# A long-convolution kernel that takes 17 of 32 magnitude columns by exponentials and the rest as products

## The chip, the cores and the metric

The kernel runs on one core of a Trainium2 chip. The core has five engines, each with its own queue of instructions that run in order: TensorE (PE, matrix products, with the weight load PEld beside it), VectorE (DVE), ScalarE (ACT, functions of single elements), GpSimd (POOL) and SyncE (SP, which issues DMAs). They wait for one another by semaphores. SBUF is the working memory with 128 partitions; PSUM takes PE's results and is read by ACT and DVE. The metric is the time of one execution in microseconds, the median of several.

## The reference

Two blocks follow each other on a sequence of 2048 tokens with 448 channels: a long convolution with a state-space kernel (S4D), and an MLP across the tokens. The change is in the making of the convolution's kernel K:

```python
dt = jnp.exp(log_dt)
A = -jnp.exp(log_A_real) + 1j * A_imag
C = (C_real + 1j * C_imag) * dt[:, None]
P = jnp.exp((A * dt[:, None])[:, :, None] * pos[None, None, :])
K = 2.0 * jnp.einsum("dn,dnl->dl", C, P).real
...
y = irfft(rfft(u_t, 2 * L) * rfft(K, 2 * L), 2 * L)[:, :, :L]
...
h = layernorm(x) * (1 + cb) + sb
u = gelu(einsum("bsd,sf->bdf", layernorm(h), w1) + b1)
x = x + gb * transpose(einsum("bdf,fs->bds", u, w2) + b2)
```

K is needed at 2048 positions for 448 channels with 256 states each. With a position written as l = 64 i + j (i below 32, j below 64) every term is a product of a factor in i and a factor in j, each with a magnitude (an exponential) and a phase (sine and cosine).

## The kernel before, in words

The states lie on the partitions. The channels are taken in 28 groups of 16, and each group in two halves of 128 states, so that there are 56 halves (`NHALF`), counted by `s`. For each half the kernel makes two magnitudes of 128 x 512 (16 channels times 32 columns): `mags[s][:, 0]` holds the powers 0 to 31 of the decay per position, and `mags[s][:, 1]`, with the coefficient in it, the 32 steps of 64 positions. `st_exponents` (L600) has PE make the exponents of both in PSUM (tiles `xe` and `xg`), as products of the parameters (`lex`) with the constant table `tab[:, 2]`; `st_exp` (L605) has ACT take the exponentials. `st_mag2` (L622) makes on POOL the powers 32 to 63 (`m2`): a small product `w` (the 32nd power, as the 31st times the first) and then `m2`, the first magnitude times `w`.

The sines and the exponentials need different tables on ACT. So the exponentials of 8 halves (`BATCH`) are taken together, in `window(s)` for s = 0, 8, 16 ... 48, and a step for each half follows. A step (`st_abs` L632, `st_phase` L611, `st_step` L639) has PE make the phases in `xe` and `xg`, ACT two absolute values and four sines (two of them into tiles of the tag `gs`, which has three buffers), POOL two products `G` of the second magnitude with sine and cosine (L650, L651), and DVE four products `E` of the first magnitude and of `m2` (L652 to L658). `st_kgen` (L672) then contracts E and G on PE.

The order on PE, ACT, DVE and POOL is the order in which this code runs, written out by hand; lists `dve` and `act` hold work that is put off to the next flush. In a window the loop over e has for each half: exponentials of half s + e, the exponents of the next, flushes, and other work. Which other work depends on the window. In those of s = 8 and 16 it is rows of the input transform (`u_rows`: PE products `pu`, then DVE products `yt`, L527) and up to five DVE steps per e from `chain` (L367, the coefficients of the coming groups, by the numbers in `WPACE`); in that of s = 24 columns of the same transform and chain steps; in those of s = 32, 40 and 48 pieces of the spectrum's product (`piece`, with `zx`, `zy` and `z` of L784 to L787), and all eight `st_mag2` of the batch. In the windows below 32 only two `st_mag2` fall into the window; the others stand in the steps. In window 0 POOL also copies `dsk` (L472).

The exponent table is built in `dft_tables` (L132 to L146) and loaded by three DMAs that POOL issues (L283).

Of the kernel before, what the change touches and what calls it, by code (L numbers as in the profile page):

```python
# [22 lines left out]
P = 128  # L23
# [16 lines left out]
def dft_tables():  # L40
# [91 lines left out]

    te = np.zeros((3, 64, 16, 32))
    tg = np.zeros((3, 16, 4, 16, 32))
    n = np.arange(32)
    for d in range(16):
        te[0, 2 * d : 2 * d + 2, d] = 2 * n + 1
        te[2, 2 * d : 2 * d + 2, d] = -n
        tg[0, d, 0:2, d] = n
        tg[0, d, 2:4, d] = 1  # L140
        tg[2, d, 0:2, d] = -64 * n
        tg[2, d, 2:4, d] = 1
    tg = tg.reshape(3, 16, 2, 2, 512).swapaxes(1, 2)
    tt = np.concatenate([te.reshape(3, 64, 512), tg.reshape(3, 64, 512)], 1)
    tt[1] = -tt[0]
    t["TT"] = tt.reshape(3, P, 512)  # L146
    return {k: np.ascontiguousarray(v.astype(np.float32)) for k, v in t.items()}
# [74 lines left out]
def tile_adaln_s4d_mixer(ctx, tc, i, out):  # L222
# [20 lines left out]
    with ExitStack() as es:  # L243
# [38 lines left out]
        tab = cg.tile([P, 3, 512], F32R, name="tab")  # L282
        for v in (2, 1, 0):  # L283
            G.dma_start(tab[:, v], i["TT"][v])
# [78 lines left out]
        def flush(todo):  # L363
            while todo:
                todo.pop(0)()
# [234 lines left out]
        def st_exponents(s):  # L600
            g, h = divmod(s, 2)
            phs[s] = [pph.tile([P, 512], F32, tag=nm, name=nm) for nm in ("xe", "xg")]
            halves(phs[s], lex[g % 4][:, h * P : (h + 1) * P], tab[:, 2], True, True)

        def st_exp(s):  # L605
            mags[s] = mp.tile([P, 2, 512], F32, tag="mag", name="mag")
            pm = phs.pop(s)
            for k in range(2):
                S.activation(mags[s][:, k], pm[k], AF.Exp)  # L609

# [11 lines left out]
        def st_mag2(s):  # L622
            me = v32(mags[s][:, 0])
            w = wp.tile([P, GD], F32, tag="w", name="w")
            G.tensor_tensor(w[:, :, None], me[:, :, 31:32], me[:, :, 1:2], ALU.mult)  # L625
            m2 = m2p[s >= 32 and s % BATCH > 2].tile([P, GD, 32], F32, tag="m2", name="m2")
            G.tensor_tensor(m2, me, w[:, :, None].to_broadcast([P, GD, 32]), ALU.mult)  # L627
            m2s[s] = m2
# [346 lines left out]
        def window(s):  # L975
# [9 lines left out]
            for e in range(BATCH):  # L985
# [10 lines left out]
                flush(act)  # L996
                flush(late_act)
                if s < 32:
                    more(WPACE[s // 8][e])
# [435 lines left out]
```

## Time and profile before

| | |
|---|---|
| median of 3 runs | 693.01 us (691.97 to 696.05) |
| the profiled execution, whole | 695.37 us |
| its span, first to last instruction | 693.2 us |
| mean granted PE clock | 0.958 |
| PE busy | 621.5 us (90%) |
| DVE busy | 456.7 us (66%) |
| ACT busy | 437.6 us (63%) |
| POOL busy | 269.2 us (39%), all of it before 394 us |

The shares are means over stages with different limits. The page's view of 40 equal slices (17.3 us each; a digit is the busy share in tenths) shows where they change:

```profile
PE   0878889889988779898899989999999999999997
DVE  7578799879779468685877577776622354444431
ACT  5867599788977789999973578777422332222220
POOL 6497468259368768889766300000000000000000
```

Slices 2 to 21 hold the convolution kernel and the input transform, the next two the rest of the convolution, and from the 23rd on the MLP runs, in which POOL does nothing. What the exponentials cost stands in the view by groups (line, engine, operation, tile, count | busy us in total, mean ns of one | idle time of the engine before them, and what ended it):

```profile
L609 ACT ACTIVATE mag<-xg 128x512 f32<-128x512 f32 x56 | 35.9, 641 | 1.2 <-PE xe L598 1.2
L609 ACT ACTIVATE mag<-xe 128x512 f32<-128x512 f32 x56 | 35.7, 637 | 15.1 <-PE xe L598 6.2 <-PE pu L524 4.1 <-POOL w L625 2.0
```

Durations of neighbours on one engine overlap by some 0.1 us; the time that an instruction takes in its queue is read from one start to the next.

### The profile page before, as it was taken

To read this page: it belongs to the slowest core of one execution; us is meant where nothing else is said; L and a number is where in the kernel's file an instruction comes from. 1 tells how busy PE (TensorE), PEld (TensorE's weight loads), DVE (VectorE), ACT (ScalarE), POOL (GpSimd) and SP (SyncE) were. 2 spreads that over 40 slices of the span, in tenths; PEclk is the share of its full clock that TensorE was granted. 3 is DMA by queue.
4 is the path that set the end of the run, shared out by engine and by line. 5 is a ranking of instruction groups with operands and counts; after the bars stand their busy time and mean duration, and the time that the engine had idled before them with its cause. 6 is when DMAs were issued, how large, how long until landed. Compare 5 with 4: busy or idle time off the path is not lost. (4 is left out here: it accounts for less than half of the span.)

```text
span 693.2 us, 18255 instructions
## 1 busy us (share of the span) xinstructions
PE 621.5 (90%) x7180; PEld 462.5 (67%) x7180; DVE 456.7 (66%) x880; ACT 437.6 (63%) x876; POOL 269.2 (39%) x323
## 2 busy tenths in 40 slices
PE   0878889889988779898899989999999999999997
PEld 0444445545535556565567757778999999999996
DVE  7578799879779468685877577776622354444431
ACT  5867599788977789999973578777422332222220
POOL 6497468259368768889766300000000000000000
PEclk9997979899999989899999999999999999999999
DMA  7694646567895526444248799965674445556540
GB/s 173 195 194 110 219 163 217 208 203 233 252 298 170 156 72 159 128 132 146 84 128 261 245 269 264 243 152 149 168 242 112 141 132 160 160 159 170 167 129 27
DMA packets 104275, 121.14 MB, mean 175 GB/s; under 512 B 12858, under 2 KB 92254, under 8 KB 104062
## 3 DMA queue, kind: packets, MB, share of 16 engines
q1 hardware_dynamic: 102830, 113.92, 56.8%
q0 software_dynamic: 1360, 6.06, 4.1%
q8 instruction: 57, 0.93, 0.6%
q14 instruction: 28, 0.23, 0.1%
HBM read 84.59 MB, written 34.87 MB: 172 GB/s over the span
## 5 line engine op out<-in xcount | busy, mean ns | idle before, releaser
L207 ACT CAST whi<-w 128x896 fp32r<-128x896 f32 x64 | 59.7, 938 | 131.7 <-PE o L1402 84.6
L650 POOL TENSOR_TENSOR G<-mag,gs 128x512 f32<-128x512 f32 x56 | 72.3, 1290 | 73.2 <-ACT gs L646 70.7
L216 DVE TENSOR_TENSOR wlo<-w,whi 128x896 fp32r<-128x896 f32 x64 | 68.0, 1086 | 40.3 <-ACT whi L207 31.0
L1332 PE MATMUL acc<-h3h,whi 128*128 128x448 f32 x224 | 83.3, 372 | 1.4 <-ACT h3h L1237 1.4
L681 PEld LDWEIGHTS kg<-E,G 128*32 128x32 f32 x3584 | 59.1, 118 | 36.5 <-issue 16.4
L1334 PE MATMUL acc<-h3h,wlo 128*128 128x448 f32 x224 | 82.0, 366 | 0.0
L1333 PE MATMUL acc<-h3l,whi 128*128 128x448 f32 x224 | 81.6, 364 | 0.2 <-DVE mean L1186 0.2
L1401 PE MATMUL o<-uh,whi 128*128 128x448 f32 x224 | 81.4, 363 | 0.0
L1403 PE MATMUL o<-uh,wlo 128*128 128x448 f32 x224 | 81.2, 363 | 0.0
L1402 PE MATMUL o<-ul,whi 128*128 128x448 f32 x224 | 80.7, 360 | 0.0
L598 PE MATMUL xg<-tab,lph 64*128 64x512 f32 x112 | 67.4, 604 | 11.6 <-DVE E L658 7.2
L681 PE MATMUL kg<-E,G 128*32 128x64 f32 x3584 | 69.4, 233 | 8.9 <-issue 4.1
L598 PE MATMUL xe<-tab,lph 64*128 64x512 f32 x112 | 66.9, 600 | 9.7 <-ACT gs L647 7.0
L651 POOL TENSOR_TENSOR G<-mag,gs 128x512 f32<-128x512 f32 x56 | 71.6, 1278 | 0.0
L1405 DVE SCALAR_TENSOR_TENSOR y<-o,b,mod 128x448 f32<-128x448 f32 x16 | 11.0, 685 | 80.2 <-PE o L1403 80.2
L627 POOL TENSOR_TENSOR m<-mag,w 128x512 f32<-128x512 f32 x56 | 59.7, 1066 | 4.6 <-POOL w L625 0.3
L652 DVE TENSOR_TENSOR E<-m,xe 128x512 f32<-128x512 f32 x56 | 38.0, 679 | 28.4 <-ACT xe L645 24.5
L1332 PEld LDWEIGHTS acc<-h3h,whi 128*128 128x128 f32 x224 | 42.5, 190 | 13.6 <-ACT h L1242 6.3
L598 PE MATMUL xe<-tab,lex 64*128 64x512 f32 x56 | 32.0, 584 | 18.4 <-POOL dsk L472 17.2
L635 ACT ACTIVATE ab<-xe 128x512 f32<-128x512 f32 x56 | 34.0, 607 | 20.4 <-PE xe L598 11.2
L609 ACT ACTIVATE mag<-xe 128x512 f32<-128x512 f32 x56 | 35.7, 637 | 15.1 <-PE xe L598 6.2
L1334 PEld LDWEIGHTS acc<-h3h,wlo 128*128 128x128 f32 x224 | 42.5, 190 | 3.3
(236 smaller groups left out, 1470.3 us busy)
## 6 DMA issues: line engine op xcount, KB each, us to landing
w<-in_B_w_dram SPq DMA_DIRECT2D x64, 224.0 KB
w<-in_B_w_dram SPq DMA_DIRECT2D x32, 448.0 KB
yu_d<-yt SPq DMA_DIRECT2D x16, 448.0 KB
yi<-yu_d SPq DMA_DIRECT2D x16, 448.0 KB
us_d<-uo SPq DMA_DIRECT2D x16, 448.0 KB
u<-us_d SPq DMA_DIRECT2D x32, 224.0 KB
v_d<-vt SPq DMA_DIRECT2D x32, 224.0 KB
vt<-v_d SPq DMA_DIRECT2D x14, 448.0 KB
```

What stands on the lines that cost most here:

```text
L207: self.nc.scalar.copy(hi, w)
L216: eng.tensor_tensor(lo, w, hi.bitcast(F32), ALU.subtract)
L598: T.matmul(out[k], lhs[r], rhs[r], start=start, stop=stop)
L650: G.tensor_tensor(Gt[:, 1], mg_, v32(sg), ALU.mult)
L651: G.tensor_tensor(Gt[:, 0], mg_, v32(cg_), ALU.mult)
L681: T.matmul(kgs[g][32 * q : 32 * q + 32, m], Gt[:, c, d], E[:, c, d], start=h == 0 and c == 0 and m == 0, stop=h == 1 and c == 1, skip_grou ...
L1332: nc.tensor.matmul(acc[f], hi[:, fs], h3h[:, r], start=r == 0, stop=False)
L1333: nc.tensor.matmul(acc[f], hi[:, fs], h3l[:, r], start=False, stop=False)
L1334: nc.tensor.matmul(acc[f], lo[:, fs], h3h[:, r], start=False, stop=r == 15)
L1401: nc.tensor.matmul(o, hi[:, ks], uh[kh][:, k], start=kh == 0 and k == 0, stop=False)
L1402: nc.tensor.matmul(o, hi[:, ks], ul[kh][:, k], start=False, stop=False)
L1403: nc.tensor.matmul(o, lo[:, ks], uh[kh][:, k], start=False, stop=kh == 1 and k == 6)
```

## The change

Only columns 0 to 16 of each magnitude come from exponentials. PE makes 16 x 17 = 272 exponents instead of 512 (table `TX` in the place of the third part of `TT`), and ACT writes 17 of every 32 columns. A new function, `st_fill`, makes columns 17 to 31 of both magnitudes in one product: columns 1 to 15 times the 16th power, which is column 16 of the first magnitude. For the second magnitude, whose step is 64 positions, the 16th power is the decay over 1024 positions; column 0 of the first magnitude is used to hold it (its exponent is 1024 times the decay) until a memset puts the 1 there that belongs there. The fills stand in the window, behind the flushes of each e: on POOL in the windows of s = 8, 16 and 24 and for the odd halves of window 0, on DVE elsewhere, 28 on each. `w` becomes the square of the 16th power.

```diff
@@ dft_tables
+    tx = np.zeros((P, 16, 17))
+    k = np.arange(17)
+    for d in range(16):
+        tx[2 * d : 2 * d + 2, d] = -np.where(k > 0, k, 1024)
+        tx[64 + 2 * d : 66 + 2 * d, d] = -64 * k
+        tx[96 + 2 * d : 98 + 2 * d, d] = 1
+    t["TX"] = tx.reshape(P, 16 * 17)
...
         tab = cg.tile([P, 3, 512], F32R, name="tab")
-        for v in (2, 1, 0):
+        G.dma_start(tab[:, 2, 0 : 17 * GD], i["TX"])
+        for v in (1, 0):
             G.dma_start(tab[:, v], i["TT"][v])
...
             phs[s] = [pph.tile([P, 512], F32, tag=nm, name=nm) for nm in ("xe", "xg")]
-            halves(phs[s], lex[g % 4][:, h * P : (h + 1) * P], tab[:, 2], True, True)
+            n = 17 * GD
+            halves([t[:, 0:n] for t in phs[s]], lex[g % 4][:, h * P : (h + 1) * P], tab[:, 2, 0:n], True, True)
...
             for k in range(2):
-                S.activation(mags[s][:, k], pm[k], AF.Exp)
+                to, src = v32(mags[s][:, k])[:, :, 0:17], pm[k][:, 0 : 17 * GD]
+                S.activation(to, src.rearrange("p (d j) -> p d j", j=17), AF.Exp)
+
+        def st_fill(s, eng):
+
+            m = mags[s].rearrange("p k (d j) -> p k d j", j=32)
+            by = m[:, 0, :, 16::-16].rearrange("p d k -> p k d")
+            to, src = m[:, :, :, 17:32], m[:, :, :, 1:16]
+            eng.tensor_tensor(to, src, by[:, :, :, None].to_broadcast([P, 2, GD, 15]), ALU.mult)
+            eng.memset(m[:, 0, :, 0:1], 1.0)
...
-            G.tensor_tensor(w[:, :, None], me[:, :, 31:32], me[:, :, 1:2], ALU.mult)
+            G.tensor_tensor(w[:, :, None], me[:, :, 16:17], me[:, :, 16:17], ALU.mult)
...
                 flush(dve)
                 flush(act)
                 flush(late_act)
+                st_fill(s + e, G if 0 < s < 32 or s + e in (1, 3, 5, 7) else V)
                 if s < 32:
                     more(WPACE[s // 8][e])
```

The order of instructions moves in two places that matter. First POOL's queue in the window of s = 8, before: the rows of the input are scaled (`xt`), and w and m2 of the first two halves follow, the second pair behind two more rows.

```order
L514 TENSOR_SCALAR xt<-xt,rs,nm 128x448 x4
L625 TENSOR_TENSOR w<-mag 128x16
L627 TENSOR_TENSOR m_976<-mag,w 128x512
L514 TENSOR_SCALAR xt<-xt,rs,nm 128x448 x2
L625 TENSOR_TENSOR w<-mag 128x16
L627 TENSOR_TENSOR m_1034<-mag,w 128x512
L650 TENSOR_TENSOR G<-mag,gs 128x512
```

The same place with the change. Line numbers are those of the new file: L625 and L626 are the fill and its memset, L642 and L644 w and m2, L667 the first G.

```order
L521 TENSOR_SCALAR xt<-xt,rs,nm 128x448 x4
L625 TENSOR_TENSOR mag<-mag 128x32x15
L626 MEMSET mag 128x16
L642 TENSOR_TENSOR w<-mag 128x16
L644 TENSOR_TENSOR m_994<-mag,w 128x512
L521 TENSOR_SCALAR xt<-xt,rs,nm 128x448 x2
L625 TENSOR_TENSOR mag<-mag 128x32x15
L626 MEMSET mag 128x16
L642 TENSOR_TENSOR w<-mag 128x16
L644 TENSOR_TENSOR m_1054<-mag,w 128x512
```

A fill stands ahead of each w, and six more fills with their memsets stand between the last m2 and the first G, where nothing stood.

Second DVE's queue in the window of s = 40, before: `ks` is a small sum, zx to z are a piece of the spectrum's product, `yk` are copies out of PSUM, and the E products of half 40 end the window.

```order
L700 TENSOR_TENSOR ks<-ks,dsk 128x4
L784 TENSOR_TENSOR zx<-kx,u 128x448
L784 TENSOR_TENSOR zy<-kx,u 128x448
L786 TENSOR_TENSOR z<-zx,zy 128x224
L787 TENSOR_TENSOR z<-zx,zy 128x224
L725 COPY yk_3482<-y_4448 128x32x2x8
L725 COPY yk_3482<-y_4449 128x32x2x8
L652 TENSOR_TENSOR E<-m_4366,xe 128x16x32
```

With the change, from the fifth of the eight fills of that window on (L801 to L804 are the piece, L742 the copies):

```order
L625 TENSOR_TENSOR mag<-mag 128x32x15
L626 MEMSET mag 128x16
L801 TENSOR_TENSOR zx<-kx,u 128x448
L801 TENSOR_TENSOR zy<-kx,u 128x448
L803 TENSOR_TENSOR z<-zx,zy 128x224
L804 TENSOR_TENSOR z<-zx,zy 128x224
L625 TENSOR_TENSOR mag<-mag 128x32x15
L626 MEMSET mag 128x16
L742 COPY yk_3546<-y_4540 128x32x2x8
L742 COPY yk_3546<-y_4541 128x32x2x8
L625 TENSOR_TENSOR mag<-mag 128x32x15
L626 MEMSET mag 128x16
```

Eight fills now stand in this stretch of DVE's queue, five ahead of the piece, one ahead of the copies and two ahead of E. POOL's queue there is the same as before (w and m2 eight times, then G); each m2 now waits for DVE's fill of its half.

More of the change, by code (lines that the diff above doesn't have):

```diff
@@ L130, in dft_tables @@
     t["FL"] = ft[24:].transpose(1, 2, 0, 3, 4).reshape(4, 8 * 64)
-    te = np.zeros((3, 64, 16, 32))
-    tg = np.zeros((3, 16, 4, 16, 32))
+    te = np.zeros((2, 64, 16, 32))
+    tg = np.zeros((2, 16, 4, 16, 32))
     n = np.arange(32)
@@ L137, in dft_tables @@
         te[0, 2 * d : 2 * d + 2, d] = 2 * n + 1
-        te[2, 2 * d : 2 * d + 2, d] = -n
         tg[0, d, 0:2, d] = n
         tg[0, d, 2:4, d] = 1
[L141 to L144, printed above, removed]
+    tg = tg.reshape(2, 16, 2, 2, 512).swapaxes(1, 2)
+    tt = np.concatenate([te.reshape(2, 64, 512), tg.reshape(2, 64, 512)], 1)
     tt[1] = -tt[0]
-    t["TT"] = tt.reshape(3, P, 512)
+    t["TT"] = tt.reshape(2, P, 512)
+    tx = np.zeros((P, 16, 17))
[5 more added lines that the diff above has]
+    t["TX"] = tx.reshape(P, 16 * 17)
     return {k: np.ascontiguousarray(v.astype(np.float32)) for k, v in t.items()}
```

## The prediction

> **What bounds the kernel now.** I read the views in this order. The chain of waits comes first: it reaches back only to 393.88 us and is nearly all TensorE (PE), so the MLP runs at PE's pace, and nothing in the diff touches it. The rest of the argument lies before that. There I cut the span at the first E product of each batch of eight halves (a half is 16 channels times one state block) and at the first exponential of each window (the stretch in which a batch's exponentials are taken), and asked for the busy time per stretch:
>
> ```profile
> core 0: us, PE busy (x) PEld busy (x) DVE busy (x) ACT busy (x) POOL busy (x), PEclk, DMA share, GB/s
> 17.97:30.75 12.78, 10.93 (x31) 6.09 (x31) 5.58 (x17) 11.59 (x23) 2.89 (x6) 1.00 0.60 190
> 30.75:69.89 39.14, 29.56 (x516) 17.02 (x516) 33.19 (x67) 28.64 (x60) 33.04 (x38) 0.87 0.75 163
> 69.89:91.96 22.07, 17.92 (x214) 9.81 (x218) 17.87 (x47) 14.93 (x29) 7.17 (x10) 0.92 0.70 234
> 91.96:126.41 34.45, 31.72 (x616) 18.38 (x610) 34.25 (x58) 32.20 (x66) 28.32 (x28) 0.85 0.55 175
> 126.41:144.33 17.92, 16.49 (x221) 9.14 (x210) 14.22 (x37) 13.81 (x27) 2.54 (x4) 0.81 0.57 208
> 144.33:179.84 35.51, 32.44 (x607) 18.42 (x605) 32.53 (x51) 30.56 (x63) 28.18 (x28) 1.00 0.74 236
> 179.84:194.67 14.83, 14.06 (x166) 6.30 (x164) 8.86 (x22) 12.81 (x26) 2.85 (x4) 1.00 0.83 251
> 229.25:244.99 15.74, 12.06 (x239) 7.81 (x238) 4.88 (x10) 11.58 (x22) 10.28 (x16) 0.89 0.43 126
> 274.26:286.76 12.50, 10.96 (x180) 7.09 (x180) 4.68 (x9) 12.27 (x26) 11.85 (x19) 1.00 0.61 173
> 286.76:315.66 28.90, 25.90 (x620) 18.01 (x620) 25.65 (x43) 27.38 (x57) 23.41 (x23) 0.88 0.37 109
> 315.66:328.16 12.50, 11.01 (x182) 7.08 (x180) 4.68 (x8) 12.27 (x26) 11.85 (x19) 1.00 0.55 163
> 393.88:693.20 299.32, 292.04 (x1434) 259.38 (x1432) 149.08 (x302) 122.01 (x208) 0.00 (x0) 0.99 0.61 166
> ```
>
> The reader is to see three kinds of window. In those of halves 0, 24, 40 and 48 ScalarE (ACT) is busy 86 to 98% of the time. In those of halves 8 and 16 ACT is busy 68 and 77%, and VectorE (DVE) has the work: 17.87 of 22.07 us, and then 34.25 of 34.45 us in the eight steps behind window 8. In windows 40 and 48 GpSimd (POOL) is almost as full as ACT, 11.85 of 12.50. So the change takes work from ACT where ACT bounds four windows, and gives it to POOL and DVE, of which one or the other is already full nearby.
>
> **What goes from ACT and PE.** Each of the 112 exponentials drops from 512 to 272 columns.
>
> ```profile
> 126.41 0.57 ACT L609 ACTIVATE mag<-xe 128x512 f32<-128x512 f32 x1
> 126.88 0.58 ACT L609 ACTIVATE mag<-xg 128x512 f32<-128x512 f32 x1
> ...
> 246.31 0.60 ACT L807 COPY vt<-vv 128x224 f32<-128x224 f32 x2
> 246.78 0.63 ACT L635 ACTIVATE ab<-xe 128x512 f32<-128x512 f32 x1
> ...
> L598 PE MATMUL xe<-tab,lex 64*128 64x512 f32 x56 | 32.0, 584 | 18.4 <-POOL dsk L472 17.2 <-DVE E L653 0.7 <-ACT mag L609 0.5
> ```
>
> Durations overlap, so starts count: 0.47 us from one exponential to the next at 512 columns, and 0.47 us for two copies of 224, 0.235 each. On the line between them 272 columns take 0.275, a saving of 0.20 us: 3.2 us per window of 16, 22 us over the kernel if all of it were on the path. PE's exponent products shrink alike, from 584 ns to some 310 (272/512); as the two halves of the array run side by side this is about 8 x 0.27 = 2.2 us of PE per window. The smaller table is worth nothing: the same three DMAs are issued.
>
> **What comes on POOL and DVE.** One fill has 2 x 16 x 15 = 480 results, and a memset of 16 follows it. 28 go to POOL and 28 to DVE.
>
> ```profile
> L650 POOL TENSOR_TENSOR G<-mag,gs 128x512 f32<-128x512 f32 x56 | 72.3, 1290 | 73.2 <-ACT gs L646 70.7 <-PE xe L598 2.5
> L627 POOL TENSOR_TENSOR m<-mag,w 128x512 f32<-128x512 f32 x56 | 59.7, 1066 | 4.6 <-POOL w L625 0.3
> L316 POOL MEMSET dsk<- 128x112 f32 x1 | 0.2, 200 | 0.1
> L658 DVE TENSOR_TENSOR E<-m,xg 128x512 f32<-128x512 f32 x56 | 37.9, 676 | 0.0
> ```
>
> On POOL the nearest row is L627, which also broadcasts one input: 480/512 x 1.066 = 1.0 us, against 1.2 by L650; with at most 0.2 for the memset I take 1.2 us per fill (bounds 1.05 and 1.4). On DVE it is L658: 480/512 x 0.676 = 0.63 us, 0.75 with the memset. Neither price is yet the cost, since a fill has both inputs in SBUF and its neighbours on the other engine too. What happens then stands in the trace:
>
> ```profile
> 74.12 1.05 POOL L627 TENSOR_TENSOR m<-mag,w 128x512 f32<-128x512 f32 x1
> 74.24 1.20 DVE L380 TENSOR_TENSOR hl<-A_log_A_real,hl 128x256 fp32r<-128x256 f32 x1
> 80.94 0.42 DVE L380 TENSOR_TENSOR hl<-s,hl 128x256 fp32r<-128x256 f32 x1
> ...
> 281.40 0.24 POOL L625 TENSOR_TENSOR w<-mag 128x16 f32<-128x16 f32 x1
> 281.72 1.05 POOL L627 TENSOR_TENSOR m<-mag,w 128x512 f32<-128x512 f32 x1
> 281.82 1.20 DVE L786 TENSOR_TENSOR z<-zx,zy 128x224 f32<-128x224 f32 x1
> 282.73 0.39 POOL L625 TENSOR_TENSOR w<-mag 128x16 f32<-128x16 f32 x1
> ```
>
> The same DVE subtraction (L380) takes 0.42 us when POOL is idle and 1.20 when it starts 0.12 us into a POOL product: it is held until POOL is through, 0.78 us. In the other direction the w product of POOL behind DVE's z takes 0.39 instead of 0.24, 0.15 us for a DVE operation of 224 columns. The engines alternate, and each meeting costs one of them time.
>
> The Trainium skill has this as a rule ("SBUF — State Buffer", section "Who interferes with whom"): "A DVE instruction with two SBUF inputs contends with a GpSimd instruction that reads SBUF", and the second to issue is held for the whole instruction of the first. The first pair of rows agrees (0.78 of 1.05 us); the second shows POOL losing only 0.15 us. By the page's whole instruction POOL would lose up to 0.63 us per DVE fill instead of the 0.32 that I use below, and the sum would be some 5 us higher (8 x 0.31 in each of windows 40 and 48).
>
> **The sum, window by window.** Later rows on which it rests:
>
> ```profile
> 16.66 1.60 POOL L472 COPY dsk<-dskr 1x112 f32<-1x112 f32 x4
> 20.70 0.60 ACT L609 ACTIVATE mag<-xg 128x512 f32<-128x512 f32 x1
> 30.75 1.27 POOL L650 TENSOR_TENSOR G<-mag,gs 128x512 f32<-128x512 f32 x1 [8.49 <-ACT gs L646]
> ...
> 91.96 0.68 DVE L652 TENSOR_TENSOR E<-m,xe 128x512 f32<-128x512 f32 x1
> 144.33 0.69 DVE L652 TENSOR_TENSOR E<-m,xe 128x512 f32<-128x512 f32 x1 [1.69 <-ACT xe L645]
> ...
> 276.10 0.24 POOL L625 TENSOR_TENSOR w<-mag 128x16 f32<-128x16 f32 x1
> 285.88 1.05 POOL L627 TENSOR_TENSOR m<-mag,w 128x512 f32<-128x512 f32 x1
> 287.24 1.27 POOL L650 TENSOR_TENSOR G<-mag,gs 128x512 f32<-128x512 f32 x1 [0.32 <-ACT gs L646]
> 289.04 0.63 ACT L636 ACTIVATE gs<-xg 128x512 f32<-128x512 f32 x1
> ```
>
> *Window 0: +0.3 us.* ACT would be 3.2 us earlier, but the first G product (30.75) is also last in POOL's queue, and POOL sets the pace behind it (33.04 of 39.14 us). That queue now holds four fills, two pairs of w and m at 0.3 + 1.0, and the dsk copies (1.60), which ran before the exponentials and now stand behind two fills: 4 x 1.2 + 2.6 + 1.6 = 9.0 us, from about 20.6, when the second half's exponentials are through (20.70 + 0.60, less the saving). That gives 29.6, and with four DVE fills in between at up to 0.35 each 31.0. Bounds -1.2 and +2.
>
> *Window 8: +2.5 us.* The fills stand on POOL among DVE's coefficient steps (L378 to L447), 29 of them planned in this window, of the kind of L380. Each fill can hold one for up to 0.78 us; about half of them will meet a step rather than a yt product (DVE products with one input in PSUM, such as L658, keep their 676 ns beside a busy POOL), so I take 0.4: 8 x 0.4 = 3.2 us. The first E product behind them starts at 91.96 with no idle time before it, and DVE is full for the next 34 us, so the delay stays. PE's shorter products give back 0.7 of their 2.2 us, where DVE waits for PE at the window's head. Bounds: -1.5 (nobody held, and the shorter products all count) and 8 x 0.78 = +6.2.
>
> *Window 16: +1.5 us.* The same 3.2 us, but DVE is 1.69 us ahead of ACT at its first E product (144.33), which covers as much. Bounds -1.5 and +4.5.
>
> *Window 24: -2.0 us.* Here DVE has idle time (8.86 of 14.83 busy), and ACT is the bound. Of the 3.2 us saved POOL leaves 2: eight fills and two w and m are 8 x 1.2 + 2.6 = 12.2 us, from 0.6 us on, in a stretch of 14.83. Bounds -2.5 and +1.
>
> *Window 32: 0.* ACT (11.58 of 15.74) waits in turn for PE; POOL's queue (10.28 busy) has room for the delay of the next paragraph. Bounds -1.5 and +1.
>
> *Windows 40 and 48: +1.7 us each.* POOL multiplies w and m eight times in a row from 276.10 to 286.93 and then has 0.32 us to spare before G. An m now also waits for its fill on DVE, and eight fills interleave with this row: by the 0.15 us for 224 columns, 480 cost 0.32 each, 2.6 us, and some 0.3 before the first m. G starts 2.9 - 0.32 = 2.6 us later and ends at 291.1. ACT's absolute value (289.04) writes into the buffer that G has just read (three gs buffers, two per step), so it moves by 2.0 us whatever ACT saved; ACT's 1.5 idle us in the next 28.90 give back 0.3. Cover for the DVE fills themselves is DVE's idle time here, 4.68 of 12.50 busy. Bounds -0.5 and +4 each.
>
> Sum: 0.3 + 2.5 + 1.5 - 2.0 + 0 + 1.7 + 1.7 = **+5.7 us**. The profiled execution took 695.4 us, 693.2 of it span; 701.1 on its scale. It lies 2.4 us above the median of 693.0, so the forecast is 698.7, **699.0 us**.
>
> **Rivals.** *ACT's saving gets through.* If fills and neighbours seldom meet, only queues count: window 0 -1.2, windows 8, 16 and 32 -1.5 each, window 24 -2.5, windows 40 and 48 -0.5 each, together -9.2: 683.8, say 684. For it speaks ACT's 98% in windows 40 and 48; against it the 1.20 and 0.39 us rows. The 14.9 us between the two sums are 0.27 us of holding for each of the 56 fills; at 0.16 the change is worth nothing. Chance 0.35.
>
> *The two cancel*: holding at that break-even, 693. Chance 0.15.
>
> *The saving is not there, or the fill is dearer.* Were an exponential that writes 17 columns of every 32 as long as a full one, window 24 would be at +1 and window 0 at +2: 704. Were POOL's fill 1.6 us, the holding in windows 8 and 16 would rise by a third and window 0 by 1.6: also about 703. Chance 0.08. The forecast itself, with a range of its own from 694 to 706, has 0.42.
>
> **How the numbers follow.** The range goes from the first rival's 684 to 710, where windows 8, 16, 40 and 48 are all at their upper bounds (5.7 + 3.7 + 3.0 + 4.6 = 17 us). 0.5% is 3.5 us, about what a measurement can tell from no change. Faster by more: 0.35. Within: 0.15 and 0.03 of the forecast's lower tail, 0.18. Slower by more: 0.47.
>
> **What would show it.** Right: in windows 8 and 16 coefficient steps of 0.3 and 0.4 us take about 1.1, and the first E product comes later after the window's first exponential than the 22.07 and 17.92 us of before; in windows 40 and 48 G no longer waits for ACT but follows the last m directly, and ACT waits for POOL at the absolute value of the next step. Exponentials start 0.275 us apart. Wrong: if those two windows get shorter by 2 us or more, or if DVE's steps keep their old durations beside POOL's fills, the first rival holds. If fills on POOL take above 1.4 us, the price is wrong, not the mechanism.

## The result, and the profile after

| | before | after |
|---|---|---|
| median | 693.29 us (691.97 to 696.05, 4 runs) | 717.34 us (713.15 to 718.56, 4 runs) |
| ratio | | 1.0331, 95% interval 1.0278 to 1.0383 |
| the profiled execution, and its span | 695.37, 693.2 us | 713.15, 711.2 us |
| mean granted PE clock of it | 0.958 | 0.942 |

The change makes the kernel 3.3% slower, some 24 us where 5.7 had been forecast: the direction was right, the size far off and outside the range. The profiled execution of the kernel after was the fastest of its four, so that this pair of spans is 18.0 us apart. A second pair of profiles, from the last experiment, has spans of 695.6 and 716.3 us.

The first view is again the busy time per stretch, cut as in the prediction: windows 8, 16 and 24 from their first exponential to the first E product and the eight steps behind windows 8 and 16. The columns are the stretch and its length, busy time and instructions of PE, PEld, DVE, ACT and POOL, the granted clock, and the DMA share and rate.

```profile
69.41:98.48 29.07, 19.51 (x206) 10.75 (x210) 23.01 (x46) 13.86 (x33) 20.47 (x30) 0.80 0.52 175
98.48:135.92 37.44, 32.21 (x605) 19.43 (x603) 37.37 (x58) 30.44 (x61) 24.94 (x25) 0.86 0.50 158
135.92:158.03 22.11, 19.48 (x232) 12.06 (x225) 18.33 (x37) 11.07 (x27) 12.06 (x20) 0.64 0.43 157
158.03:196.21 38.18, 33.96 (x607) 18.76 (x605) 32.67 (x52) 30.65 (x64) 27.98 (x28) 0.96 0.72 226
196.21:212.16 15.95, 13.53 (x166) 6.52 (x164) 13.53 (x22) 10.26 (x26) 11.73 (x20) 1.00 0.63 187
```

Read the DVE column of the first three rows against before. DVE has the same instructions there (46, 58 and 37; before 47, 58 and 37), since the fills of these windows run on POOL. Yet it is busy for 23.01, 37.37 and 18.33 us instead of 17.87, 34.25 and 14.22: 12.4 us more for the same work. The stretches are longer by 7.0, 3.0 and 4.2 us, 14.2 us together, most of the 18.0 us between the two spans. The fourth row, the steps behind window 16, is 2.7 us longer with DVE busy as before (32.67 against 32.53 us). In the fifth, window 24, DVE is again busier with the same 22 instructions: 13.53 instead of 8.86 us.

From the first exponential of one window to that of the next, which leaves out nothing, the two pairs of profiles give:

| part | forecast | first pair | second pair |
|---|---|---|---|
| up to window 0, and window 0 with its steps | +0.3 | -0.5 | -1.6 |
| window 8 with its steps | +2.5 | +10.0 | +10.5 |
| window 16 with its steps | +1.5 | +6.9 | +6.8 |
| window 24 with its steps | -2.0 | +0.4 | +4.5 |
| window 32 with its steps | 0 | -2.7 | -2.6 |
| window 40 with its steps | +1.7 | +0.4 | +1.2 |
| window 48 to the end | +1.7 | +3.5 | +1.7 |
| sum | +5.7 | +18.0 | +20.7 |

(First pair: the first exponentials start at 17.97, 69.89, 126.41, 179.84, 229.25, 274.26 and 315.66 us before, and at 16.81, 69.41, 135.92, 196.21, 246.04, 288.38 and 330.21 after.) Windows 8 and 16 make 17 us of either sum.

The groups of the kernel after (line, engine, operation, tiles, count, then busy time, mean ns of one, and idle time ahead) show which durations were right:

```profile
L644 POOL TENSOR_TENSOR m<-mag,w 128x512 f32<-128x512 f32 x56 | 63.4, 1131 | 7.8 <-DVE mag L626 2.4 <-DVE E L675 1.4
L625 POOL TENSOR_TENSOR mag<-mag 128x480 f32<-128x480 f32 x28 | 30.8, 1099 | 19.9 <-ACT mag L618 19.9
L625 DVE TENSOR_TENSOR mag<-mag 128x480 f32<-128x480 f32 x28 | 25.7, 918 | 1.6 <-ACT mag L618 1.1
L618 ACT ACTIVATE mag<-xe 128x272 f32<-128x272 f32 x56 | 23.9, 427 | 24.1 <-PE pu L531 8.0 <-PE xg L605 6.8 <-PE xe L605 5.3
```

POOL's fill takes 1.10 us, and 1.22 us pass from one fill with its memset to the next (79.97 to 81.19 us), where 1.2 was priced. DVE's takes 0.92 where 0.63 was priced, and the m product 1.13 where it took 1.07: both are held at times. ACT's exponentials are shorter as expected, but ACT now waits 24.1 us ahead of them, a third of it for TensorE's `pu`.

Where DVE's time went in window 8 is read from its timeline, and that of POOL beside it (start, duration, engine, line, operation):

```profile
82.42 1.27 DVE L387 TENSOR_TENSOR hl<-s,hl 128x256 fp32r<-128x256 f32 x1
89.52 1.02 DVE L385 CAST hl<-p 128x256 fp32r<-128x256 f32 x1
91.45 1.19 DVE L444 TENSOR_TENSOR xa<-xa,u 128x256 f32<-128x256 f32 x1
94.71 1.38 DVE L385 CAST hl<-xa 128x256 fp32r<-128x256 f32 x1
96.12 1.37 DVE L387 TENSOR_TENSOR hl<-xa,hl 128x256 fp32r<-128x256 f32 x1
97.42 1.14 DVE L534 TENSOR_TENSOR yt<-pu,mod 128x448 f32<-128x448 f32 x2
101.89 1.38 DVE L397 TENSOR_TENSOR ya<-ya,xa 128x256 f32<-128x256 f32 x1
```

```profile
82.36 1.05 POOL L625 TENSOR_TENSOR mag<-mag 128x480 f32<-128x480 f32 x1
89.08 1.31 POOL L625 TENSOR_TENSOR mag<-mag 128x480 f32<-128x480 f32 x1 [3.75 <-ACT mag L618]
91.31 1.05 POOL L625 TENSOR_TENSOR mag<-mag 128x480 f32<-128x480 f32 x1 [0.69 <-ACT mag L618]
94.67 1.27 POOL L667 TENSOR_TENSOR G<-mag,gs 128x512 f32<-128x512 f32 x1 [2.13 <-ACT gs L663]
95.90 1.31 POOL L668 TENSOR_TENSOR G<-mag,gs 128x512 f32<-128x512 f32 x1
```

The first three steps start within a fill and end 0.15 to 0.28 us behind it: this is the holding of the prediction. The next two, at 94.71 and 96.12, are held by no fill but by two G products. Before, the last of these steps ended at 90.97 us, 1.1 us ahead of the first G:

```profile
90.55 0.42 DVE L380 TENSOR_TENSOR hl<-xa,hl 128x256 fp32r<-128x256 f32 x1
92.08 1.28 POOL L650 TENSOR_TENSOR G<-mag,gs 128x512 f32<-128x512 f32 x1 [14.02 <-ACT gs L646]
```

Delayed by the fills, these two steps now run into G and lose 1.0 us each. It goes on behind the window: the product at 101.89 took 0.42 us before. And two of the five held rows are casts, with one input, of 0.29 us each before.

In window 40 the first G product follows the last m directly, as the prediction had it, and ACT waits for POOL, though at another instruction. The rows are the last m, the first G, and a sine of the next step:

```profile
303.04 1.05 POOL L644 TENSOR_TENSOR m<-mag,w 128x512 f32<-128x512 f32 x1
304.05 1.27 POOL L667 TENSOR_TENSOR G<-mag,gs 128x512 f32<-128x512 f32 x1
305.35 0.60 ACT L663 ACTIVATE gs<-xg 128x512 f32<-128x512 f32 x1 [1.45 <-POOL G L667]
```

G follows the last m at once, 15.67 us after the window's first exponential instead of 12.98: 2.7 us later, where 2.6 had been worked out. In window 48 it is 3.5 us. The absolute value of the next step (L653) waits for nothing and starts ahead of G, at 302.82 us; the wait that had been forecast there stands at the next step's sine into `gs` (L663), 1.45 us here and 3.15 us in window 48.

### The profile page after: what moved, and what is told of

It is laid out like the page before. It is cut to its first block, busy times and chain, and to the rows that moved or that the text cites. A ratio compares the mean times of both kernels' runs of the same rounds, so it can differ in the third digit from the quotient of the medians.

```text
span 711.2 us, 18386 instructions
## 1 busy us (share of the span) xinstructions
PE 621.2 (87%) x7180; PEld 465.9 (66%) x7180; DVE 501.3 (70%) x936; ACT 418.6 (59%) x876; POOL 310.6 (44%) x379
## 5 line engine op out<-in xcount | busy, mean ns | idle before, releaser
L667 POOL TENSOR_TENSOR G<-mag,gs 128x512 f32<-128x512 f32 x56 | 72.0, 1285 | 30.7 <-ACT gs L663 27.2
L698 PE MATMUL kg<-E,G 128*32 128x64 f32 x3584 | 71.0, 237 | 12.8 <-POOL G L668 6.0
L644 POOL TENSOR_TENSOR m<-mag,w 128x512 f32<-128x512 f32 x56 | 63.4, 1131 | 7.8 <-DVE mag L626 2.4
L674 DVE TENSOR_TENSOR E<-mag,xg 128x512 f32<-128x512 f32 x56 | 38.0, 678 | 9.3 <-ACT xg L665 9.3
L1351 PEld LDWEIGHTS acc<-h3l,whi 128*128 128x128 f32 x224 | 42.4, 189 | 3.1 <-DVE h3l L1262 0.5
```

The source lines that it names most:

```text
L667: G.tensor_tensor(Gt[:, 1], mg_, v32(sg), ALU.mult)
L698: T.matmul(kgs[g][32 * q : 32 * q + 32, m], Gt[:, c, d], E[:, c, d], start=h == 0 and c == 0 and m == 0, stop=h == 1 and c == 1, skip_grou ...
L1351: nc.tensor.matmul(acc[f], hi[:, fs], h3l[:, r], start=False, stop=False)
```

## Experiments

Besides the theory of holding (A) there were rivals: that every fill costs the same wherever it stands, that TensorE's shorter products lower its granted clock, and that queues rather than holding make the loss. All times are medians; ratios are to the kernel before on the same chip, with 95% intervals.

**Which windows.** The kernel after with the change limited to windows in a set `SX`, the others with the full exponentials of before. (In these kernels one DVE operation of 16 columns sets the table's first column between such windows, and the exponent product has 288 columns, not 272.)

```diff
+            if s // BATCH * BATCH not in SX:
+                halves(phs[s], lex[g % 4][:, h * P : (h + 1) * P], tab[:, 2], True, True)
+                return
...
+                if s // BATCH * BATCH not in SX:
+                    S.activation(mags[s][:, k], pm[k], AF.Exp)
+                    continue
...
-                st_fill(s + e, G if 0 < s < 32 or s + e in (1, 3, 5, 7) else V)
+                if s in SX:
+                    st_fill(s + e, G if 0 < s < 32 or s + e in (1, 3, 5, 7) else V)
```

`mid`, SX = (8, 16).

> The fills stand only in windows 8 and 16; all other windows take the full exponentials of before. Theory A (the coefficient steps): in the profiles the kernel after falls 10.0 us behind in window 8 and its steps and 6.9 us in window 16 and its steps, nearly all of its loss, because GpSimd's fills hold VectorE's coefficient steps and stand ahead of the modulated input in GpSimd's queue. Then this kernel keeps the loss: 693 + 17, so 708 to 716 us. Rival B (every fill costs about the same, 24 us / 56 = 0.43 us, wherever it stands): 16 fills, 7 us, 700 us. Rival C (a loss in one window only moves work that the others would have waited for, so that windows don't add up): below 700.

707.04 us, ratio 1.0194 (1.0131 to 1.0257).

`late`, SX = (32, 40, 48).

> The fills stand only in windows 32, 40 and 48. Theory A: in the profiles these three windows sum to -2.7 + 0.4 + 3.5 = +1.2 us, so 692 to 697 us. Rival B (0.43 us for each fill anywhere): 24 fills, 10 us, 703 us.

702.27 us, ratio 1.011 (1.0062 to 1.0157).

`edge`, SX = (0, 24).

> The fills stand only in windows 0 and 24. Theory A: -0.5 and +0.4 us in the profiles, but window 24 was entered late in the kernel after, so its own saving of 2 us may show: 690 to 694 us. Rival B: 16 fills, +7, 700 us.

698.03 us, ratio 1.0026 (0.9984 to 1.0069).

`w24`, SX = (24,).

> Fills in window 24 alone, the one window for which the prediction saw a gain (-2.0 us): by it 692 us. By the runs so far, in which no window gained: 694 to 697 us.

696.38 us, ratio 1.004 (1.001 to 1.007).

The three sets add up: 1.94 + 1.1 + 0.26 = 3.3%, the whole of the change's loss, though each term has an interval of some 0.5% to either side. Most of it is in windows 8 and 16, as theory A has it, and the rival of an equal price falls: a fill costs 0.84 us there (13.5 us for 16), 0.32 in the late windows (7.6 for 24) and 0.11 in windows 0 and 24 (1.8 for 16). But `mid` came out 1 us under A's range, `late` and `edge` 5 and 4 us over theirs; and window 24, the one with a forecast gain, has none.

**Fills left out.** Exponentials of 17 columns, no fill and no memset; the magnitude tiles are eight fixed ones, in which columns 17 to 31 keep what an earlier half wrote.

```diff
-                st_fill(s + e, G if 0 < s < 32 or s + e in (1, 3, 5, 7) else V)
...
+        ring = [mp.tile([P, 2, 512], F32, tag="mag%d" % k, name="mag", bufs=1) for k in range(8)]
...
-            mags[s] = mp.tile([P, 2, 512], F32, tag="mag", name="mag")
+            mags[s] = ring[s % 8]
```

`mid_nofill`.

> Windows 8 and 16 take exponentials of 17 columns, but their 16 fills and memsets are left out (columns 17 to 31 keep what an earlier half wrote there); all other windows as before. The kernel with these fills took 12.7 us more than before. Theory A (the fills make the loss: their time, what they hold and what stands behind them): without them at or below before, 690 to 694 us. Rival B (shorter exponentials themselves cost time, since TensorE's shorter products leave it idle and its granted clock falls: 8 us more of half speed were lost in that kernel than before): most of the loss stays, 700 us or more.

697.76 us, ratio 1.0024 (0.9987 to 1.0062).

`late_nofill`.

> The same for windows 32, 40 and 48: exponentials of 17 columns, the 24 fills left out. With the fills this kernel took 8 us more than before. Theory A: without them below before, by ScalarE's saving of up to 3.2 us in each of windows 40 and 48, so 686 to 691 us. Rival B: above before, 697 us or more.

694.12 us, ratio 0.9998 (0.9969 to 1.0027).

`all_nofill`, windows 8 to 48.

> Exponentials of 17 columns in windows 8 to 48 and no fill at all (columns 17 to 31 keep what an earlier half wrote there): what ScalarE's shorter exponentials and TensorE's shorter products are worth when the rest costs nothing. Theory A (they are worth nothing, since VectorE, GpSimd and TensorE set the pace of these windows, as the two kernels without fills showed in windows 8 and 16 and in 32 to 48): 692 to 698 us. Rival C (the saving of 3.2 us per window was there, and shows in window 24 at least): 688 us or less.

691.71 us, ratio 1.0002 (0.9965 to 1.0039).

So the loss is the fills', as theory A says; without them it is gone. But nor is there a gain: even with fills that cost nothing, shorter exponentials in windows 8 to 48 bring at most 0.35% (2.4 us). While the rest of the order stays as it is, no arrangement of these fills can be expected to beat the kernel before by more than that. Window 40 of `all_nofill` shows why there:

```profile
284.16 1.27 POOL L677 TENSOR_TENSOR G<-mag,gs 128x512 f32<-128x512 f32 x1
```

G follows the last m (283.16 us, 1.05 long) at once, 13.21 us after the window's first exponential (12.98 before): with ACT relieved, POOL's row of w and m sets its start.

**The clock.** `pe512`: as after, but TensorE makes 512 columns of exponents and ACT reads 17 of every 32.

```diff
-            halves([t[:, 0:n] for t in phs[s]], lex[g % 4][:, h * P : (h + 1) * P], tab[:, 2, 0:n], True, True)
+            halves(phs[s], lex[g % 4][:, h * P : (h + 1) * P], tab[:, 2], True, True)
```

> The kernel after, but TensorE's exponent products keep their 512 columns as before, and ScalarE reads 17 of every 32 from them; fills as in the kernel after. Rival B (TensorE's idle time and its granted clock make the loss): the clock's mean goes back from 0.94 to 0.95 or more, and the time falls from 717 to 705 us or less. Theory A: TensorE has 2.2 us more per window, partly beside waits: 717 to 722 us.

715.31 us, ratio 1.0308 (1.0245 to 1.0371), granted clock 0.942 in the profile: the same as after. `mid_nofill`, with the shorter products and no loss, has 0.961 where before has 0.958. The rival of the shorter products falls.

**What holds, in windows 8 and 16.** `midV`: the 16 fills of `mid` on DVE.

```diff
-                    st_fill(s + e, G if 0 < s < 32 or s + e in (1, 3, 5, 7) else V)
+                    st_fill(s + e, V)
```

> As the kernel with fills in windows 8 and 16 alone, but these 16 fills run on VectorE, not on GpSimd. Theory A: nothing on GpSimd is there to hold a coefficient step or to stand ahead of the modulated input; VectorE has 0.65 + 0.07 us more per fill, 5.8 us per window, of which 2 to 4 us fit into its idle time: +2 to +4 us per window, 697 to 701 us, well below the kernel with GpSimd's fills. Rival B: the fill itself costs the time on either engine, so the same as that kernel.

713.1 us, ratio 1.0279 (1.0207 to 1.0351): no faster than with POOL's fills (the two intervals overlap), although POOL's queue is here that of before. The expectation was wrong, and the reason is in the table below.

`mid_mem`: POOL writes the 480 results twice by a memset, which reads nothing; columns 17 to 31 hold 0.5.

```diff
-            eng.tensor_tensor(to, src, by[:, :, :, None].to_broadcast([P, 2, GD, 15]), ALU.mult)
+            for _ in range(2):
+                eng.memset(to, 0.5)
```

> Windows 8 and 16 with 17 columns, and in the place of each product of 480 on GpSimd two memsets of the same 480 results, which read nothing (columns 17 to 31 are wrong). Theory A1 (what costs is that the product and VectorE's coefficient steps hold each other over SBUF): with nothing read on GpSimd the steps keep their 0.3 to 0.4 us and the time falls to that of the kernel without fills. Theory A2 (what costs is GpSimd's queue, where the modulated input stands behind the fills): if two memsets take about 1 us, the time stays at that of the kernel with fills, 705 to 709 us.

700.15 us, ratio 1.0091 (1.0059 to 1.0124). The two memsets take 1.04 us, as long as the product, so POOL's queue is the same; the difference to `mid`, 1.0%, goes with 7.8 us less of holding in DVE's busy time, as the table below has it. Neither expected time came: 0.7% more than in `mid_nofill` remains, and this run does not part what one-input steps still lose from what POOL's queue costs. DVE's steps in the middle of the window, with memsets on POOL throughout:

```profile
81.38 0.57 DVE L386 CAST hl<-s 128x256 fp32r<-128x256 f32 x1
81.98 0.43 DVE L388 TENSOR_TENSOR hl<-s,hl 128x256 fp32r<-128x256 f32 x1
82.32 0.69 DVE L425 TENSOR_SCALAR ph<-A_A_imag,dt 128x256 f32<-128x256 f32 x1
```

The subtraction with two inputs keeps its 0.43 us; the cast and the tensor-scalar step, with one input, are held (0.28 and 0.34 before).

`mid_split`: two products of 240 on POOL in the place of one of 480.

```diff
-            eng.tensor_tensor(to, src, by[:, :, :, None].to_broadcast([P, 2, GD, 15]), ALU.mult)
+            for k in range(2):
+                eng.tensor_tensor(to[:, k], src[:, k], by[:, k, :, None].to_broadcast([P, GD, 15]), ALU.mult)
```

> Windows 8 and 16 with GpSimd's fills as two products of 240 in the place of one of 480. Theory A' (a VectorE step that meets a GpSimd instruction waits for the end of this one instruction, as the steps beside memsets of 0.5 us did, which took 0.57 to 0.69 us in the place of 0.28 to 0.34): the steps are held half as long, and the time falls from 707 to 701 to 704 us, though GpSimd needs some 0.2 us more per fill. Rival E (a step waits until GpSimd's queue runs empty, or the queue's length is what counts): 707 us or more.

707.39 us, ratio 1.0176 (1.0123 to 1.0229): no gain. Single holds are shorter in the trace (0.59 to 0.84 us beside fills), as expected, but there are more of them, and the pair takes POOL 1.2 to 1.5 us. The expected 701 to 704 us did not come; by its time alone this run would also fit rival E, the length of POOL's queue, which `midV` speaks against.

What joins these five kernels is DVE's busy time. The view by stretch, for window 8 with its steps and window 16 with its steps, of before, `mid_nofill`, `mid_mem`, `mid_split`, `mid` and `midV` in turn:

```profile
69.89:126.41 56.52, 49.64 (x816) 28.19 (x820) 52.12 (x103) 47.13 (x93) 35.49 (x38) 0.88 0.61 198
126.41:179.84 53.43, 48.93 (x826) 27.56 (x814) 46.75 (x88) 44.37 (x89) 30.72 (x32) 0.94 0.68 227
```

```profile
71.28:131.24 59.96, 50.87 (x850) 29.41 (x850) 51.66 (x103) 44.20 (x92) 35.80 (x38) 0.83 0.54 180
131.24:183.11 51.87, 44.99 (x781) 25.26 (x778) 46.54 (x88) 41.26 (x90) 30.58 (x32) 1.00 0.71 233
```

```profile
69.53:130.40 60.87, 49.38 (x850) 28.18 (x850) 54.77 (x103) 44.17 (x92) 45.21 (x64) 0.89 0.56 183
130.40:186.85 56.45, 49.36 (x781) 27.57 (x778) 48.53 (x88) 41.38 (x90) 38.18 (x54) 0.91 0.65 216
```

```profile
69.80:134.55 64.75, 52.39 (x850) 30.33 (x850) 58.58 (x103) 44.46 (x93) 46.95 (x62) 0.82 0.53 172
134.55:192.53 57.98, 51.00 (x780) 28.27 (x778) 49.56 (x88) 41.59 (x90) 41.69 (x56) 0.88 0.64 210
```

```profile
68.65:133.52 64.87, 50.04 (x850) 29.26 (x850) 58.78 (x103) 44.48 (x92) 45.27 (x54) 0.87 0.52 170
133.52:189.82 56.30, 49.63 (x781) 27.84 (x778) 52.36 (x88) 41.49 (x89) 40.25 (x48) 0.88 0.67 215
```

```profile
71.93:139.72 67.79, 52.70 (x798) 30.44 (x802) 62.26 (x119) 44.40 (x92) 36.84 (x38) 0.82 0.49 159
139.72:199.92 60.20, 52.45 (x839) 29.37 (x830) 53.39 (x105) 41.70 (x90) 30.30 (x32) 0.87 0.62 202
```

| kernel | DVE busy in both, over before | time over before, by its ratio |
|---|---|---|
| `mid_nofill` | -0.7 us | +1.7 us |
| `mid_mem` | +4.4 us | +6.3 us |
| `mid_split` | +9.3 us | +12.2 us |
| `mid` | +12.3 us | +13.5 us |
| `midV` | +16.8 us, of it 11.9 the fills' own | +19.4 us |

All but `midV` have the 103 and 88 DVE instructions of before, so their surplus is holding alone. In the four kernels with a surplus, each us that DVE is busy longer in these windows comes with 1.1 to 1.4 us of time, whether it is held or has more to do; the times are known to some 2 to 5 us. That is why the fills on DVE were no cure: 16 x (0.67 + 0.07) = 11.9 us of its own, and 4.9 us of holding still, since the delayed steps meet POOL's m and G products.

**Windows 32 to 48.** `late_psum`: ACT writes the 16th powers of a half (32 columns) into the free end of the exponents' PSUM bank, and the DVE fill reads them there, so that it has one input in SBUF.

```diff
-            by = m[:, 0, :, 16::-16].rearrange("p d k -> p k d")
+            by = bys.pop(s)
...
+                bys[s] = pm[0][:, 480:512].rearrange("p (k d) -> p k d", d=GD)
+                src = pm[0][:, 0 : 18 * GD].rearrange("p (d j) -> p d j", j=18)[:, :, 16::-16]
+                S.activation(bys[s], src.rearrange("p d k -> p k d"), AF.Exp)
```

> Windows 32, 40 and 48 with fills on VectorE, but the 16th power that a fill multiplies by is written by ScalarE to PSUM (one more exponential of 32 columns per half), so that the fill has one input in SBUF and one in PSUM, like the E products, which keep 0.68 us beside a busy GpSimd. Theory A (holding: VectorE's fill and GpSimd's w and m product wait for each other): a fill keeps 0.65 us, w keeps 0.24 us, and the time falls from 702 to 694 to 697 us. Rival D (the fills cost by standing in VectorE's queue ahead of z and yk, for which TensorE waits): 700 us or more.

710.54 us, ratio 1.0238 (1.0194 to 1.0281). The groups of `late`, and then of `late_psum`, from window 32 on (m, fill, w):

```profile
L653 POOL TENSOR_TENSOR m<-mag,w 128x512 f32<-128x512 f32 x25 | 29.8, 1191 | 4.5 <-DVE mag L635 2.8
L634 DVE TENSOR_TENSOR mag<-mag 128x480 f32<-128x480 f32 x24 | 22.4, 932 | 2.5 <-ACT mag L627 1.7 <-issue 0.3
L651 POOL TENSOR_TENSOR w<-mag 128x16 f32<-128x16 f32 x24 | 10.2, 426 | 0.5 <-ACT mag L627 0.5
```

```profile
L659 POOL TENSOR_TENSOR m<-mag,w 128x512 f32<-128x512 f32 x24 | 25.1, 1048 | 9.2 <-DVE mag L641 7.1 <-DMA lex<-pars 0.9
L640 DVE TENSOR_TENSOR mag<-mag,xe 128x480 f32<-128x480 f32 x24 | 15.5, 649 | 7.0 <-ACT mag L633 6.5
L657 POOL TENSOR_TENSOR w<-mag 128x16 f32<-128x16 f32 x24 | 5.6, 233 | 2.1 <-ACT mag L633 2.1
```

With one input in PSUM nobody is held: the fill takes 0.65 instead of 0.93, w 0.23 instead of 0.43, m 1.05 instead of 1.19. But the edit brought a wait of its own: TensorE's next exponents now wait for the fill to free the bank (11.0 us in 12 waits in its view of waits between 228 and 350 us). So the time says nothing on the price of the holding. `late_kg` put the powers in the unused half of the bank of `kg` instead:

```diff
+        kgbank = pkg.tile([P, 512], F32, tag="kg", name="kg")
...
+                c = 256 + 32 * (s % 8)
+                bys[s] = kgbank[:, c : c + 32].rearrange("p (k d) -> p k d", d=GD)
```

> Windows 32, 40 and 48 with fills on VectorE; the 16th power that they multiply by is written by ScalarE to the unused half of the PSUM bank of kg, so that no exponent product waits for a fill. Theory A (VectorE's fill and GpSimd's w and m hold each other): fills 0.65 us, w 0.24, m 1.05, TensorE no longer waits for the bank, and the time falls from 702 to 694 to 697 us. Rival D (the queue): fills are short, but the time stays at 700 us or more.

716.68 us, ratio 1.0295 (1.0231 to 1.036): waits of the edit's own again. In window 40 ACT's write to that bank waits 0.31 to 1.52 us, for DVE or TensorE, and exponentials of successive halves start 1.6 us apart. Inconclusive too.

`late_yk`: the two yk copies of a window go from DVE to ACT.

```diff
-                    st_s1(s > 16)
+                    st_s1(16 < s < 32)
```

> Windows 32, 40 and 48 with fills on VectorE as in the kernel after; the two yk copies of a window go to ScalarE, which the shorter exponentials have relieved by 3.2 us, so that they stand behind no fill. Theory A: TensorE's waits for yk were a consequence of held fills; most of the loss stays, 699 to 702 us. Rival D: TensorE's 5.5 us of waits for yk go, 695 to 698 us.

701.73 us, ratio 1.0116 (1.0076 to 1.0155), as `late`. What TensorE waited for between 228 and 350 us (us in total, times, longest), in `late` and then in `late_yk`:

```profile
PE vv L827 <- DVE yk L751: 5.5, 3, 1.9
PE kg L707 <- POOL G L677: 2.5, 4, 1.2
```

```profile
PE xe L606 <- ACT ab L661: 6.7, 2, 3.4
PE kg L707 <- POOL G L677: 4.3, 5, 1.5
```

The 5.5 us of waits for yk are gone, and as much time is waited for ab and G instead. That the row of w and m on POOL stands behind these waits is the likely reading; it is not shown. `late_kgyk`, both edits:

> Both edits. If holding and queue add up: 692 to 695 us, the time without any fill (694). By the runs without fills it can't be below that by more than the measurement tells.

713.96 us, ratio 1.0271 (1.0221 to 1.0322), no more telling than `late_kg`.

**How far single profiles agree.** Unchanged kernels a second time.

> The kernel with fills in windows 32, 40 and 48 a second time, unchanged. In its first profile window 32 began at 235.21 us (229.25 before), 6.0 us late, with TensorE's clock at half speed in other places than before, though the instructions up to there are the same. Theory P (the half-speed stretches fall anew in each execution, so that a single profile has some 2 to 6 us of chance in it): window 32 begins elsewhere, 229 to 237 us, and the sum of the three windows stays at 2 to 4 us above before. Theory Q (the offset belongs to the kernel): it begins at 235 us again. Time 700 to 704 us under either.

700.31 us, ratio 1.0105 (1.0061 to 1.0148); window 32 began at 232.57 us, and from there to the end the profile took 464.4 us (466.4 in the first).

> The kernel before a second time. Theory P: window 8 takes 56.5 to 60.4 us and window 16 53.4 to 57.5, as in the eight profiles of kernels that are unchanged there; window 32 begins at 229 to 236 us. Theory Q: the same starts as in the first profile within 0.5 us.

693.42 us, ratio 0.9975 (0.9935 to 1.0016); window 32 began at 231.22 us (229.25), and from there 464.4 us (464.0).

> The kernel after a second time; its first profile was the fastest of four executions. Both theories: 714 to 719 us; windows 8 and 16 with their steps again 64 to 68 and 58 to 61 us, since every profile with fills there had the first at 64.7 or more.

715.3 us, ratio 1.0318 (1.025 to 1.0386); windows 8 and 16 with their steps took 68.2 and 60.3 us.

So the start of window 32 moves by 2.0 and 2.6 us between two executions of one kernel, in the kernel after by 5.5 (246.04 and 251.58), and differences of that size in one profile mean nothing. Thirteen profiles have no fill in windows 8 and 16. In them these windows with their steps took 56.2 to 60.4 and 51.9 to 57.5 us, while DVE's busy time in both together was 98.1 to 99.0 us. So the busy time is the firm measure, and the 17 us of length, taken against two of the four shortest of the thirteen, are nearer to 15 against their mean.

Window 8 took 64.7 us or more in all six profiles with fills there, longer than in any of the thirteen (and 60.9 with the memsets). Window 16 is less sure: `pe512` had DVE as busy there as the kernel after (50.96 and 51.00 us, 46.75 before) and took 55.1 us, the kernel after 60.3, with granted clocks of 0.91 and 0.84. A part of the 6.9 us of window 16 is therefore not holding; how much is not settled.

For the late windows there is a gap: `late` is slower by 1.1% in both measurements, 7.5 us, but from window 32 on its two profiles took only 2.4 and 0.0 us longer than the two of before. Against `late_nofill`, which has the same exponentials and no fills, they took 8.9 and 6.9 us longer (457.5 us from window 32 on), much as by the medians; but that profile entered window 32 as late as the first of `late` (235.34 and 235.21 us), and why is not settled.

## Why the prediction was right or wrong

*The bounds.* Right: ACT in windows 0, 24, 40 and 48, DVE in 8 and 16, POOL in 40 and 48. It was not drawn far enough. Where POOL is as full as ACT (11.85 of 12.50 us), ACT's saving is worth no more than the 0.32 us of slack, as window 40 of `all_nofill` shows; that nothing is gained in windows 8 to 48 together is shown by its time (1.0002). The rival "ACT's saving gets through" had a chance of 0.35 and rested on savings of up to 2.5 us in a window; with fills that cost nothing, 8.0 of its 9.2 us would have been there in these windows, and at most 2.4 are.

*Prices of the new instructions.* Right on POOL (1.10 us, memset 0.15). The exponentials start 0.28 us apart, as forecast. On DVE the fill's own price was right where nothing holds it (0.65 us in `late_psum`, 0.63 forecast).

*Windows 8 and 16, +2.5 and +1.5.* Here the prediction failed, by a term that was mis-sized: "about half of them will meet a step rather than a yt product", 8 x 0.4 = 3.2 us. Measured as DVE's busy time for the same instructions, the holding is 8.3 us in window 8 and its steps (23.01 + 37.37 against 17.87 + 34.25) and 4.1 in window 16 (18.33 against 14.22). So the term was short by more than half in window 8; in window 16 it was nearly right, and the cover of 1.69 us failed. Three things were left out. A step held by a fill is late for the next, and steps that slip past the window meet POOL's G products, which hold them for longer than a fill; the upper bound of 8 x 0.78 stopped at the window's end. Steps with one input are held too, about half of all steps; only those with two had been thought of. And what was given back (0.7 us of TensorE's time in window 8, the 1.69 us lead of DVE in window 16) did not come back: 14.2 us of length for 12.4 of holding. Of the 6.9 us of window 16 and its steps a part is not holding but goes with a lower granted clock (0.84, against 0.91 in `pe512`), and for that the prediction had no term. In the other term, "DVE is full for the next 34 us, so the delay stays", the prediction was right for window 8, and the table of five kernels agrees.

The Trainium skill ("SBUF — State Buffer", "Who interferes with whom") would have given the second point: it states that copy, cast and tensor-scalar operations can, when their operands allow it, enter a mode with two ports and then contend with GpSimd, while an operation with two SBUF inputs contends only with GpSimd's reads. The trace agrees on both: a cast of 0.29 us took 1.38 beside G and 0.57 beside a memset, the subtraction 1.37 beside G and 0.43 beside memsets. The prediction had read only the half on two inputs.

*Window 24, -2.0.* Wrong: no gain with fills there alone (+0.1 to +0.7%). Two steps failed. The credit for ACT is absent even without fills: in `all_nofill` the first E product comes 15.46 us after the window's first exponential, 14.83 before. And "DVE has idle time" put the holding at nothing, while POOL's eight fills kept DVE busy 13.53 instead of 8.86 us with the same 22 instructions; the E product, which had waited 2.50 us for ACT, now follows DVE's last step at once.

*Windows 32, 40 and 48, 0, +1.7 and +1.7.* The mechanism held for POOL: G 2.7 and 3.5 us later, straight behind the last m; moving the yk copies away changed nothing. ACT's wait was one step off: not the absolute value but the next step's sine into `gs` waited for G (1.45 and 3.15 us). The price that POOL pays to a DVE fill was right too: w and m together took 0.43 + 1.19 us in `late` and 0.23 + 1.05 without holding, 0.34 us for each fill, against the 0.32 of the prediction and the 0.63 of a hold for the whole instruction. The sum of the parts, +3.4, lies between the profiles of `late` (0.0 and +2.4) and its medians (+7.5); which is nearer is open.

*Window 0, +0.3.* The first G product came at 29.12 us, 1.6 earlier than before, of which 1.2 are the earlier start of the exponentials (16.81 against 17.97); this stretch ended 0.5 and 1.6 us ahead.

## What to carry to other kernels

Ask of every engine in the stretch whether it is as full as the one that is relieved: work taken from an engine whose neighbour has the same length of work is worth only the slack between them, here nothing. Idle time of an engine is not proof against holding: window 24 used it up. Where two engines hold each other, price the delay by the busy time of the engine that bounds the stretch, and follow each delayed instruction to what it will meet next, past the end of the stretch in which the change stands. The busy time of one engine for an unchanged number of instructions is a quick measure of holding, and here a steady one: it varied by 0.9 us where the length of the stretch varied by 4.

## What the runs showed of the hardware that had not been expected

A DVE cast or tensor-scalar step of 0.28 to 0.34 us with a single SBUF input is held by POOL like one with two, up to 1.38 us, and it is held (0.57 and 0.69 us) even beside a POOL memset, which reads nothing and leaves the two-input subtraction at 0.43.

The same instructions can take visibly different time in two executions: window 24 with its steps took 49.83 and 53.99 us in the two profiles of the kernel after, with granted clocks of 0.93 and 0.87. Below is window 16 with its steps in `late_nofill` and before, which agree there but for the buffers of the magnitudes, in stretches of 14 us; the row shown is the third of each:

```profile
154.00:168.00 14.00, 11.49 (x153) 6.27 (x153) 13.62 (x22) 7.74 (x16) 10.96 (x13) 0.76 0.57 179
```

```profile
154.40:168.40 14.00, 12.49 (x231) 7.27 (x233) 14.00 (x24) 10.66 (x22) 12.51 (x14) 1.00 0.68 219
```

The granted clock is 0.76 in the one and 1.00 in the other, and the whole of this part took 57.46 instead of 53.43 us. The Trainium skill ("TensorE: Matmul & The Clock Gate", "What's actually happening") states that the clock follows the array's activity in windows of about 3.4 us that run freely, so that the program does not set where they fall. The trace agrees: in stretches of 1 us the clock is 0.50 from 161 to 167 us, and the half-speed time by the mean, 2 x 0.24 x 14 = 6.7 us, is two such windows.
